# All 32 later output blocks in pairs of seven half products, and early units placed anew, in a fused attention and bilinear FFN kernel

## The chip, the cores and the metric

One core of one Trainium2 chip. The metric is device time in microseconds (us) of one execution of the whole kernel; the median of several runs is quoted. The profile is one execution, whose span (first to last instruction) is 1.7 to 1.8 us shorter than the time. All verdicts use runs of state fast.

## The reference, cut to what matters

```python
# q, k, v: (8 batches, 8 heads, 576, 64); phi: (8, 8, 576, 32); all f32
a = softmax(phi, axis=seq)                       # 32 memory slots per head
k_m, v_m = a^T k, a^T v                          # (32, 64) per head
attn = softmax(q k_m^T / 8) v_m
x = attn rearranged to (4608 tokens, 512)
out = ((x @ w_a) * (x @ w_b)) @ w_out            # d_ff = 1536; out: (4608, 512) f32
```

## The kernel before

Attention is never formed: v_m is folded into w_a and w_b for each batch (`fold`, tiles `pva` to `vab`), so that the two up projections (`pa`, `pb`) take the normalised scores `A` directly. ScalarE copies `pa` out, DVE multiplies it by `pb` into `ht` (f16). The down product takes `ht` in 36 blocks of 128 tokens. Four early ones are plain (12 products of 512 columns each, `po`). Later ones go in pairs: a pair of blocks, with d_ff and d_model halved, is a 2x2 times 2x2 block product that needs seven half products in place of eight, on sums of `ht` (`h_sums`, GpSimd or DVE) and of w_out (`w_sums`):

```python
def two_downs(self, cidx):                       # (cut to its order)
    y: a11*B11 -> u1      v: S1*T1 -> u5
    y += S2*T2 -> u2      v += S4*B22;  o1[:, NH:] = v + u2     (DVE)
    y += S3*T3;           o2[:, NH:] = y + u5                   (DVE)
    x: a12*B21;           o1[:, :NH] = x + u1                   (DVE), store o1
    y += a22*T4;          o2[:, :NH] = y                        (ACT), store o2
# each of the seven: 6 matmuls of 256 columns (KH = 6)
```

The last two blocks were left out of the pairs: block 34 is plain, block 35 is `last_down`, in two halves of 12 products of 256 columns, each stored as soon as it is ready, through SyncE and ScalarE:

```python
PAIRED = range(EARLY + PLAIN, BLOCKS - 2, 2)     # 15 pairs: blocks 4 to 33
def products(self):                              # (cut)
    for cidx in PAIRED[:-1]: yield from two_downs(self, cidx)
    yield from down(BLOCKS - 2)
    yield from two_downs(self, PAIRED[-1])
...
work.pull(work.ready - work.done)
last_down(B // 2 * NI - 1)
```

The chain of the next batch (`exp`, sums over k and v `ks vs` or `kv`, transposes `kt vt` or `kvt`, scores `sc`, `den`, `nr`, folds `v0 v1 v2` and their copies `x0 x1 x2`) is cut into units, and strings say in which slot (between two up products) each unit is issued; `a` and `b` are the folds of w_a and w_b, `hv` are half folds, `y3` is three early down products:

```python
ups(steps(0, 0, 4), slots(0, "- hv1a+hx1a - hv1b+hx1b - v1a+x1a - v1b+x1b"))
load(2)
ups(steps(0, 4, 12), slots(0, "- - - - v2a+x2a - v2b+x2b"))
chain(1, "exp0 exp1 y9 ks0 y3 kt0 qt0 qt1 y1 ks1 y3 kt1 s0 e0 ... y1 hv0a hx0a y2 hv0b hx0b y2")
```

Folds, sums, scores and the transposes of k and v run in tiled form (64 x 32, 32 x 32 or 128 x 32 of the array), ups and downs on the full array. Tiled work between full-array products is called an island below.

The softmax here doesn't subtract the row's maximum and nothing guards it: scores larger than these inputs give would overflow.

Of the kernel before, what the change touches and what calls it, by code (L numbers as in the profile page):

```python
# [8 lines left out]
F32 = mybir.dt.float32  # L9
F16 = mybir.dt.float16  # L10
AF = mybir.ActivationFunctionType
ALU = mybir.AluOpType

P = 128
# [4 lines left out]
def kernel(  # L19
# [381 lines left out]
    def down(cidx):  # L401

        po, bank = banks.take([P, d_model], F32, "po", hold=True)
        yield from down_part(po, bank, cidx, 0, NFF)

    def last_down(cidx):

        pair, c = divmod(cidx, NI)
        w = d_model // 2
        for x in range(2):  # L410
            cs = slice(w * x, w * (x + 1))
            po = banks.tile([P, w], F32, name="pl")
            o_sb = opool.tile([P, w], F32, name="o_sb")
            for i in range(NFF):
                nc.tensor.matmul(po, ht[:, i, P * c:P * (c + 1)], wo_sb[:, i, cs],
                                 start=(i == 0), stop=(i == NFF - 1))
            nc.scalar.mul(out=o_sb[:, :w // 2], in_=po[:, :w // 2], mul=1.0 / (CS * CS))
            nc.vector.tensor_scalar(out=o_sb[:, w // 2:], in0=po[:, w // 2:], scalar1=1.0 / (CS * CS), scalar2=None,
                                    op0=ALU.mult)
            for z, engine in enumerate((nc.sync, nc.scalar)):  # L420
                slot = 2 * c + z
                engine.dma_start(out=out_rows[2 * pair + slot // NI, slot % NI, :, cs],
                                 in_=o_sb[64 * z:64 * z + 64, :])

    EARLY = 4

    def early_downs():
# [28 lines left out]
    def sum_tokens(cidx, engine):  # L456

        h_sums[cidx] = spool.tile([P, 4, KH, P], F16, name="h_sums")
        t = [h_sums[cidx][:, x] for x in range(4)]
        (a11, a12), (a21, a22) = ([tokens_of(cidx + y, x) for x in range(2)] for y in range(2))  # L460
        for out, in0, in1, op in ((t[0], a21, a22, ALU.add), (t[1], t[0], a11, ALU.subtract),
                                  (t[2], a12, t[1], ALU.subtract), (t[3], a11, a21, ALU.subtract)):
            engine.tensor_tensor(out=out, in0=in0, in1=in1, op=op)  # L463
            yield

    def store(o_sb, cidx):
        pair, c = divmod(cidx, NI)
        for z in range(2):
            slot = 2 * c + z
            nc.sync.dma_start(out=out_rows[2 * pair + slot // NI, slot % NI], in_=o_sb[64 * z:64 * z + 64, :])  # L470

    def two_downs(self, cidx):
        S1, S2, S4, S3 = (h_sums[cidx][:, x] for x in range(4))
        T1, T2, T3, T4 = (w_sums[:, x] for x in range(4))
        (a11, a12), (a21, a22) = ([tokens_of(cidx + y, x) for x in range(2)] for y in range(2))
        scale = 1.0 / (CS * CS)

        def products(po, lhs, rhs, first=False):
            for i in range(KH):
                nc.tensor.matmul(po, lhs[:, i], rhs[:, i], start=first and i == 0,  # L480
                                 stop=i == KH - 1, skip_group_check=not first)
                if i < KH - 1:
                    yield

        def part(po, name):
            x = ppool.tile([P, NH], F32, name=name)
            nc.scalar.mul(out=x, in_=po, mul=scale)
            return x

        def plus(o, po, x):  # L490
            nc.vector.scalar_tensor_tensor(out=o, in0=po, scalar=scale, in1=x, op0=ALU.mult, op1=ALU.add)

        o1, o2 = (opool.tile([P, d_model], F32, name="o_sb") for _ in range(2))
        y, ybank = banks.take([P, NH], F32, "py", hold=True)
        yield from products(y, a11, quarter(0, 0), True)
        u1 = part(y, "u1")
        yield
        v, vbank = banks.take([P, NH], F32, "pv", hold=True)
        self.brim = True
        yield from products(v, S1, T1, True)  # L500
        u5 = part(v, "u5")
        yield
        yield from products(y, S2, T2)
        u2 = part(y, "u2")
        yield
        yield from products(v, S4, quarter(1, 1))
        banks.free(vbank)
        plus(o1[:, NH:], v, u2)
        self.brim = False
        yield  # L510
        yield from products(y, S3, T3)
        plus(o2[:, NH:], y, u5)
        yield
        x, xbank = banks.take([P, NH], F32, "px", hold=True)
        self.brim = True
        yield from products(x, a12, quarter(1, 0), True)
        banks.free(xbank)
        plus(o1[:, :NH], x, u1)
        store(o1, cidx)
        self.brim = False  # L520
        yield
        yield from products(y, a22, T4)
        banks.free(ybank)
        nc.scalar.mul(out=o2[:, :NH], in_=y, mul=scale)
        store(o2, cidx + 1)
        yield

    BLOCKS = B // 2 * NI
    LEAD = 24
    PLAIN = 0  # L530
    PAIRED = range(EARLY + PLAIN, BLOCKS - 2, 2)

    class Work:

# [7 lines left out]
            self.next_sum = next(self.sums)  # L542

        def products(self):
            for cidx in range(EARLY, EARLY + PLAIN):
                yield from down(cidx)
            for cidx in PAIRED[:-1]:
                yield from two_downs(self, cidx)
            yield from down(BLOCKS - 2)
            yield from two_downs(self, PAIRED[-1])  # L550

        def add_up(self):
            for n, cidx in enumerate(PAIRED):
                for x in range(4):
                    yield n, NFF * PLAIN + 7 * KH * n + KH * (x + 1)
                    if x == 0:
                        sums = sum_tokens(cidx, nc.gpsimd if n < len(PAIRED) - 1 else nc.vector)
                    next(sums)
            while True:
                yield len(PAIRED), 0  # L560

# [21 lines left out]
        def plan(self, tokens, slots, keep=24):  # L583

            n = min(max(0, tokens // P - PAIRED[0]) // 2, len(PAIRED))
            self.summed = n
            self.ready = NFF * min(PLAIN, tokens // P - EARLY) + 7 * KH * n + NFF * (tokens // P >= BLOCKS - 1)
            self.rate = max(0, self.ready - self.done - keep) / slots
            self.owed = 0.0
            self.sum_ahead()  # L590
# [27 lines left out]
    def ups(steps, side=()):  # L618

        side = iter(side)  # L620
        for step in steps:
            for _ in up(*step):
                work.advance()
                next(side, us[step[0]]["-"])()
        for f in side:
            work.advance()
            f()

    def steps(b, lo, hi):

        return [(b, i, (0, 1)) for i in range(lo, hi)]
# [37 lines left out]
    def chain(b, plan):  # L669


        for x in plan.split():
            if x[0] == "f":
                fill(int(x[1:]), 256)
            elif x[0] == "y":
                some(int(x[1:]))
            else:
                us[b][x]()
# [1 line left out]
    fill(16)  # L680
    chain(0, "exp0 exp1 ks0 f3 kt0 qt0 qt1 f14 s0 e0 ks1 f3 kt1 qt2 qt3 f6 den0 f4 s1 nr0 e1 f6 vs0 vs1 vt0 vt1 den1 f3 "
             "hv0a hx0a nr10 nr11 hv0b hx0b f4")
    ups(steps(0, 0, 4), slots(0, "- hv1a+hx1a - hv1b+hx1b - v1a+x1a - v1b+x1b"))
    load(2)
    ups(steps(0, 4, 12), slots(0, "- - - - v2a+x2a - v2b+x2b"))
    chain(1, "exp0 exp1 y9 ks0 y3 kt0 qt0 qt1 y1 ks1 y3 kt1 s0 e0 qt2 qt3 y6 den0 y2 s1 e1 nr0 y4 den1 y2 vs0 vs1 y1 vt0 vt1 nr1 y1 hv0a hx0a y2 hv0b hx0b y2")
    load(3)
    sum_weights()
    ups(steps(1, 0, 4), slots(1, "y1 hv1a+hx1a hv1b+hx1b y1 v1a+x1a v1b+x1b y3 y3"))
    ups(half_steps(1, 0, 4), slots(1, "- v2a+x2a+v2b+x2b+qt0' - exp0' - exp1'+qt1' - qt2'+kv'+km'+y9"))  # L690
    work.plan(S + HALF, 10)
    ups(half_steps(1, 1, 4), slots(2, "qt3 kvt - sc+e0+e1+den0 - nr0+den1+v0+x0a - - x0b+nr1 - v1+x1b+x1a -"))
    second = "v2_+x2a_+exp0 x2b_ - exp1 qt0+kv+km - qt1+kvt+qt2 qt3 sc+e0 - e1+v0+x0a x0b den0+v1+x1a nr0+L x1b+exp0' den1 - nr1+v2+x2a - x2b+exp1' qt0' kv'+qt1' km' - qt2'+kvt'+qt3'"
    every = "- sc+e0 e1 den0 v0+x0a+x0b - - nr0 exp0' - v1+x1a x1b+qt0' den1 - exp1' v2+x2a+x2b nr1+qt1' - kv'+km' qt2' kvt'+qt3' L - -"
    last = "sc+e0 - e1 - v0 x0b den1+x0a - den0 - nr0+v1+x1a nr1 x1b - - - - - - v2+x2a - - - x2b"
    for b in range(2, B):
        if b == 2:
            load(4)
# [4 lines left out]
            ups(half_steps(b, hf), side[NFF * hf:NFF * (hf + 1)] if hf == 0 else side[NFF:])  # L703
    work.plan(S * B, 1, 0)
    work.pull(work.ready - work.done)
    last_down(B // 2 * NI - 1)
# [1 line left out]
_INS = ['q', 'k', 'v', 'phi', 'moe_w_a', 'moe_w_b', 'moe_w_out']  # L708
_OUTS = [((4608, 512), 'float32')]
# [25 lines left out]
```

## Time and profile before

| | before |
|---|---|
| time, median of 3 | 247.81 us (247.73 to 247.85) |
| span of the profile | 246.4 us |
| first up product of batch 0 | 20.45 us |
| first up product of batch 1 | 49.63 us |
| last up product starts | 228.70 us |
| last down product ends | 242.14 us |
| last store lands | 245.28 us |

The positions are read from the timeline: the first `pa` row of a batch, the last `pb` row, and for the end the `pl` row (239.36 + 2.78) and the last store's issue with its time to landing.

### The profile page before, as it was taken

To read this page: it belongs to the slowest core of one execution; us is meant where nothing else is said; L and a number is where in the kernel's file an instruction comes from. 1 tells how busy PE (TensorE), PEld (TensorE's weight loads), DVE (VectorE), ACT (ScalarE), POOL (GpSimd) and SP (SyncE) were. 2 spreads that over 40 slices of the span, in tenths; PEclk is the share of its full clock that TensorE was granted. 3 is DMA by queue.
4 is the path that set the end of the run, shared out by engine and by line. 5 is a ranking of instruction groups with operands and counts; after the bars stand their busy time and mean duration, and the time that the engine had idled before them with its cause. 6 is when DMAs were issued, how large, how long until landed. Compare 5 with 4: busy or idle time off the path is not lost.

```text
span 246.4 us, 7681 instructions
## 1 busy us (share of the span) xinstructions
PE 234.4 (95%) x3049; PEld 167.1 (68%) x3049; DVE 166.5 (68%) x401; ACT 157.9 (64%) x409; POOL 151.1 (61%) x123
## 2 busy tenths in 40 slices
PE   7589999999998999999999999999999999999993
PEld 3354574456655857777787777877787787888782
DVE  3636794477959967876994649865995686756620
ACT  2247772578697489578856768588855877565330
POOL 8724233499799029892899759892849186936000
PEclk9999999999999999999999999999999999999999
DMA  6999999999979804973159732695120303033145
GB/s 198 210 198 206 211 252 207 255 220 271 233 183 207 160 4 108 238 127 85 33 149 208 174 85 45 167 207 145 32 56 3 88 7 82 10 78 71 43 104 128
DMA packets 26036, 33.82 MB, mean 137 GB/s; under 512 B 1936, under 2 KB 20368, under 8 KB 26000
## 3 DMA queue, kind: packets, MB, share of 16 engines
q0 software_dynamic: 19280, 22.71, 50.3%
q1 hardware_dynamic: 6288, 9.90, 16.3%
q10 hardware_dynamic: 432, 0.72, 0.8%
q8 instruction: 24, 0.39, 0.6%
q14 instruction: 12, 0.10, 0.1%
HBM read 42.47 MB, written 9.44 MB: 211 GB/s over the span
## 4 chain that ended last, share of the span: by engine, by line
PE 74%; DMA 17%; DVE 3%; POOL 2%; ACT 1%; issue 1%; ACTq 0%; DVEq 0%; POOLq 0%
PE pa L602 18%; PE pb L612 16%; PE py L480 15%; PE pv L480 8%; DMA phi_sb<-in_phi_dram 6%; DMA wo_sb<-in_moe_w_out_dram 6%; DMA wb_sb<-in_moe_w_b_dram 5%; PE pva L337 5%; PE px L480 4%; PE po L389 3%; PE pkv L213 2%; PE pD L314 1%; PE pscore L292 1%; PE pT L242 1%; POOL q_sb L90 1%
## 5 line engine op out<-in xcount | busy, mean ns | idle before, releaser
L615 DVE TENSOR_TENSOR ht<-a_sb,pb 128x288 f16<-128x288 f16 x192 | 82.9, 448 | 40.2 <-ACT a_sb L605 29.3
L605 ACT CAST a_sb<-pa 128x288 f16<-128x288 f32 x192 | 74.7, 405 | 31.6 <-PE pa L602 31.0
L602 PE MATMUL pa<-A,vab 128*128 128x288 f16 x384 | 76.5, 287 | 1.4 <-DVE A L325 1.4
L612 PE MATMUL pb<-A,vab 128*128 128x288 f16 x384 | 76.5, 286 | 0.2
L463 POOL TENSOR_TENSOR h_sums<-ht 128x768 f16<-128x768 f16 x28 | 45.9, 1640 | 34.0 <-DVE ht L615 34.0
L612 PEld LDWEIGHTS <-vab 128*128 128x128 f16 x384 | 37.0, 98 | 13.2 <-issue 1.9
L602 PEld LDWEIGHTS <-vab 128*128 128x128 f16 x384 | 34.5, 98 | 15.9 <-issue 9.1
L480 PEld LDWEIGHTS <-h_sums 128*128 128x128 f16 x360 | 35.1, 98 | 6.5 <-issue 0.4
L349 ACT CAST vab<-pva 128x512 f16<-128x512 f32 (+1 forms) x52 | 28.1, 558 | 10.0 <-PE pva L337 10.0
L349 DVE CAST vab<-pva 128x512 f16<-128x512 f32 (+1 forms) x52 | 32.8, 643 | 2.4 <-PE pva L337 2.0
L480 PEld LDWEIGHTS <-ht 128*128 128x128 f16 x270 | 26.4, 98 | 5.4 <-issue 0.2
L480 PE MATMUL py<-w_sums,h_sums 128*128 128x256 f16 x180 | 28.5, 272 | 0.0
L463 POOL TENSOR_TENSOR h_sums<-h_sums,ht 128x768 f16<-128x768 f16 x14 | 23.1, 1650 | 1.0
L463 POOL TENSOR_TENSOR h_sums<-ht,h_sums 128x768 f16<-128x768 f16 x14 | 23.0, 1642 | 1.0
L305 ACT ACTIVATE E<-pscore 128x288 f16<-128x288 f32 x32 | 11.4, 416 | 13.6 <-PE pscore L292 13.5
L325 POOL TENSOR_TENSOR A<-E,R 128x576 f16<-128x576 f16 x10 | 12.8, 1278 | 11.9 <-ACT R L323 11.6
L389 PE MATMUL po<-wo_sb,ht 128*128 128x512 f16 x60 | 16.0, 381 | 0.1
L480 PE MATMUL py<-wo_sb,ht 128*128 128x256 f16 x90 | 15.2, 273 | 0.0
L480 PE MATMUL pv<-w_sums,h_sums 128*128 128x256 f16 x90 | 15.2, 273 | 0.0
L204 DVE STREAM_TRANSPOSE qT<-q_sb 128x288 f32<-128x288 f32 x32 | 14.5, 463 | 0.6 <-DMA q_sb<-in_q_dram 0.6
L480 PE MATMUL py<-w_sums,ht 128*128 128x256 f16 x90 | 14.7, 272 | 0.1
L315 ACT ACTIVATE L<-pD 128x288 f32<-128x288 f32 x32 | 11.4, 413 | 5.0 <-PE pD L314 4.8
(66 smaller groups left out, 273.1 us busy)
## 6 DMA issues: line engine op xcount, KB each, us to landing
out_dram<-o_sb SPq DMA_DIRECT2D x70, 128.0 KB, 2.4
kv_sb<-in_v_dram POOLq DMA_DIRECT2D x7, 576.0 KB, 10.5
phi_sb<-in_phi_dram POOLq DMA_DIRECT2D x7, 576.0 KB, 4.6
kv_sb<-in_k_dram POOLq DMA_DIRECT2D x7, 576.0 KB, 8.2
q_sb<-in_q_dram POOLq DMA_DIRECT2D x6, 576.0 KB, 12.8
wo_sb<-in_moe_w_out_dram POOLq DMA_DIRECT2D x3, 512.0 KB, 17.4
q_sb<-in_q_dram POOLq DMA_DIRECT2D x4, 288.0 KB, 12.7
wa_sb<-in_moe_w_a_dram POOLq DMA_DIRECT2D x2, 512.0 KB, 14.8
```

What stands on the lines that cost most here:

```text
L204: nc.vector.transpose(out=t["qT"][:, hp, :].bitcast(F32), in_=qs[b][:, hp, :].bitcast(F32))
L305: nc.scalar.activation(out=Ev[:, g, :, z, :], in_=pss, func=AF.Exp, scale=1.0 / (8.0 * CS))
L325: engine.tensor_tensor(out=attn[b][:, g, sl], in0=t["E"][:, g, sl], in1=t["R", g][:, sl], op=ALU.mult)
L337: nc.tensor.matmul(t["pva", lo, z][g][0][32 * j:32 * j + 32, 0:hi - lo], t["kvT"][64 * r:64 * r + 64, 4 + g, M * j:M * j + M], w_sbs[z][64 ...
L349: engine_copy(out=vabs[b][z][:, g, lo:hi], in_=pva[:, 0:hi - lo])
L389: nc.tensor.matmul(po, ht[:, i, P * c:P * (c + 1)], wo_sb[:, i, :], start=(i == 0), stop=(i == NFF - 1))
L463: engine.tensor_tensor(out=out, in0=in0, in1=in1, op=op)
L480: nc.tensor.matmul(po, lhs[:, i], rhs[:, i], start=first and i == 0, stop=i == KH - 1, skip_group_check=not first)
L602: nc.tensor.matmul(pa, vab[0][:, g, fs], A[:, g, HALF * hf:HALF * (hf + 1)], start=(g == 0), stop=(g == 1))
L605: nc.scalar.copy(out=a_sb, in_=pa)
L612: nc.tensor.matmul(pb, vab[1][:, g, fs], A[:, g, HALF * hf:HALF * (hf + 1)], start=(g == 0), stop=(g == 1))
L615: nc.vector.tensor_tensor(out=ht[:, i, t0:t0 + HALF], in0=a_sbs[hf - hfs[0]], in1=pb, op=ALU.mult)
```

## The change

The intent: put the last two blocks into a sixteenth pair (48 products' worth becomes 42); let DVE sum the last two pairs; store the last pair in pieces; and place the early units anew, so that fewer tiled islands stand between full-array products and TensorE has work while inputs arrive. The diff, cut to its core:

```diff
-    def last_down(cidx):
-        ... (24 half-width products, four small stores)
-    def store(o_sb, cidx):
+    def store(o_sb, cidx, cs=slice(0, d_model), engines=(nc.sync, nc.sync)):
...
         plus(o2[:, NH:], y, u5)
+        if ends:                                   # ends: the last pair
+            store(o2, cidx + 1, slice(NH, d_model))
...
         nc.scalar.mul(out=o2[:, :NH], in_=y, mul=scale)
+        if ends:
+            store(o2, cidx + 1, slice(0, NH), (nc.sync, nc.scalar))
...
-    PAIRED = range(EARLY + PLAIN, BLOCKS - 2, 2)
+    PAIRED = range(EARLY, BLOCKS, 2)
-                        sums = sum_tokens(cidx, nc.gpsimd if n < len(PAIRED) - 1 else nc.vector)
+                        sums = sum_tokens(cidx, nc.gpsimd if n < len(PAIRED) - 2 else nc.vector)
...
-    ups(steps(0, 0, 4), slots(0, "- hv1a+hx1a - hv1b+hx1b - v1a+x1a - v1b+x1b"))
+    ups(steps(0, 0, 4), slots(0, "hv1a+hv1b hx1b+hx1a - - - v1a+x1a v1b x1b"))
-    ups(steps(0, 4, 12), slots(0, "- - - - v2a+x2a - v2b+x2b"))
+    ups(steps(0, 4, 12), slots(0, "- - - - v2a+x2a+v2b+x2b - -"))
-    chain(1, "... y1 ks1 y3 kt1 s0 e0 qt2 qt3 y6 den0 y2 s1 e1 nr0 y4 den1 y2 vs0 vs1 y1 vt0 vt1 nr1 y1 hv0a hx0a y2 hv0b hx0b y2")
+    chain(1, "... y1 y3 ks1 qt2 s0 e0 y6 kt1 qt3 den0 y3 s1 nr0 e1 y4 y2 den1 vs0 vs1 vt0 y1 vt1 nr1 hv0a hx0a hv0b y3 hx0b y2")
...  (slots of batches 2 to 7: units moved by one or two slots)
```

More of the change, by code (lines that the diff above doesn't have):

```diff
@@ L404, in down @@
         yield from down_part(po, bank, cidx, 0, NFF)
-    def last_down(cidx):
-        pair, c = divmod(cidx, NI)
-        w = d_model // 2
-        for x in range(2):
-            cs = slice(w * x, w * (x + 1))
-            po = banks.tile([P, w], F32, name="pl")
-            o_sb = opool.tile([P, w], F32, name="o_sb")
-            for i in range(NFF):
-                nc.tensor.matmul(po, ht[:, i, P * c:P * (c + 1)], wo_sb[:, i, cs],
-                                 start=(i == 0), stop=(i == NFF - 1))
-            nc.scalar.mul(out=o_sb[:, :w // 2], in_=po[:, :w // 2], mul=1.0 / (CS * CS))
-            nc.vector.tensor_scalar(out=o_sb[:, w // 2:], in0=po[:, w // 2:], scalar1=1.0 / (CS * CS), scalar2=None,
-                                    op0=ALU.mult)
-            for z, engine in enumerate((nc.sync, nc.scalar)):
-                slot = 2 * c + z
-                engine.dma_start(out=out_rows[2 * pair + slot // NI, slot % NI, :, cs],
-                                 in_=o_sb[64 * z:64 * z + 64, :])
     EARLY = 4
@@ L469, in store @@
             slot = 2 * c + z
-            nc.sync.dma_start(out=out_rows[2 * pair + slot // NI, slot % NI], in_=o_sb[64 * z:64 * z + 64, :])
+            engines[z].dma_start(out=out_rows[2 * pair + slot // NI, slot % NI, :, cs], in_=o_sb[64 * z:64 * z + 64, cs])
     def two_downs(self, cidx):
@@ L476, in two_downs @@
         scale = 1.0 / (CS * CS)
+        ends = cidx == PAIRED[-1]
         def products(po, lhs, rhs, first=False):
@@ L524, in two_downs @@
         nc.scalar.mul(out=o2[:, :NH], in_=y, mul=scale)
-        store(o2, cidx + 1)
+        if ends:
+            store(o2, cidx + 1, slice(0, NH), (nc.sync, nc.scalar))
+        else:
+            store(o2, cidx + 1)
         yield
@@ L529 @@
     LEAD = 24
-    PLAIN = 0
-    PAIRED = range(EARLY + PLAIN, BLOCKS - 2, 2)
+    PAIRED = range(EARLY, BLOCKS, 2)
     class Work:
@@ L544, in products @@
         def products(self):
-            for cidx in range(EARLY, EARLY + PLAIN):
-                yield from down(cidx)
-            for cidx in PAIRED[:-1]:
+            for cidx in PAIRED:
                 yield from two_downs(self, cidx)
-            yield from down(BLOCKS - 2)
-            yield from two_downs(self, PAIRED[-1])
         def add_up(self):
@@ L554, in add_up @@
                 for x in range(4):
-                    yield n, NFF * PLAIN + 7 * KH * n + KH * (x + 1)
+                    yield n, 7 * KH * n + KH * (x + 1)
                     if x == 0:
-                        sums = sum_tokens(cidx, nc.gpsimd if n < len(PAIRED) - 1 else nc.vector)
+                        sums = sum_tokens(cidx, nc.gpsimd if n < len(PAIRED) - 2 else nc.vector)
                     next(sums)
@@ L586, in plan @@
             self.summed = n
-            self.ready = NFF * min(PLAIN, tokens // P - EARLY) + 7 * KH * n + NFF * (tokens // P >= BLOCKS - 1)
+            self.ready = 7 * KH * n
             self.rate = max(0, self.ready - self.done - keep) / slots
@@ L682 @@
              "hv0a hx0a nr10 nr11 hv0b hx0b f4")
-    ups(steps(0, 0, 4), slots(0, "- hv1a+hx1a - hv1b+hx1b - v1a+x1a - v1b+x1b"))
+    ups(steps(0, 0, 4), slots(0, "hv1a+hv1b hx1b+hx1a - - - v1a+x1a v1b x1b"))
     load(2)
-    ups(steps(0, 4, 12), slots(0, "- - - - v2a+x2a - v2b+x2b"))
-    chain(1, "exp0 exp1 y9 ks0 y3 kt0 qt0 qt1 y1 ks1 y3 kt1 s0 e0 qt2 qt3 y6 den0 y2 s1 e1 nr0 y4 den1 y2 vs0 vs1 y1 vt0 vt1 nr1 y1 hv0a hx0a y2 hv0b hx0b y2")
+    ups(steps(0, 4, 12), slots(0, "- - - - v2a+x2a+v2b+x2b - -"))
+    chain(1, "exp0 exp1 y9 ks0 y3 kt0 qt0 qt1 y1 y3 ks1 qt2 s0 e0 y6 kt1 qt3 den0 y3 s1 nr0 e1 y4 y2 den1 vs0 vs1 vt0 y1 vt1 nr1 hv0a hx0a hv0b y3 hx0b y2")
     load(3)
     sum_weights()
-    ups(steps(1, 0, 4), slots(1, "y1 hv1a+hx1a hv1b+hx1b y1 v1a+x1a v1b+x1b y3 y3"))
-    ups(half_steps(1, 0, 4), slots(1, "- v2a+x2a+v2b+x2b+qt0' - exp0' - exp1'+qt1' - qt2'+kv'+km'+y9"))
+    ups(steps(1, 0, 4), slots(1, "- hv1a+hx1a hv1b+hx1b+y1 - v1a+x1a y3+v1b x1b y3"))
+    ups(half_steps(1, 0, 4), slots(1, "- v2a+x2a+v2b+x2b+qt0' - - qt1'+exp0'+qt2' exp1' - kv'+km'+y9"))
     work.plan(S + HALF, 10)
-    ups(half_steps(1, 1, 4), slots(2, "qt3 kvt - sc+e0+e1+den0 - nr0+den1+v0+x0a - - x0b+nr1 - v1+x1b+x1a -"))
-    second = "v2_+x2a_+exp0 x2b_ - exp1 qt0+kv+km - qt1+kvt+qt2 qt3 sc+e0 - e1+v0+x0a x0b den0+v1+x1a nr0+L x1b+exp0' den1 - nr1+v2+x2a - x2b+exp1' qt0' kv'+qt1' km' - qt2'+kvt'+qt3'"
-    every = "- sc+e0 e1 den0 v0+x0a+x0b - - nr0 exp0' - v1+x1a x1b+qt0' den1 - exp1' v2+x2a+x2b nr1+qt1' - kv'+km' qt2' kvt'+qt3' L - -"
-    last = "sc+e0 - e1 - v0 x0b den1+x0a - den0 - nr0+v1+x1a nr1 x1b - - - - - - v2+x2a - - - x2b"
+    ups(half_steps(1, 1, 4), slots(2, "- kvt qt3 sc+e0+e1+den0 - nr0+den1+v0+x0a - - x0b+nr1 - v1+x1b x1a"))
+    second = "v2_+x2a_+exp0 x2b_ exp1 - qt0+kv+km - qt1+qt2 kvt+qt3 sc+e0 - e1+v0+x0a den0+x0b v1+x1a nr0+L x1b+exp0' den1 - nr1+v2+x2a - x2b+exp1' - qt0'+kv'+qt1' km' - qt2'+kvt'+qt3'"
+    every = "- sc+e0 e1 den0 v0+x0a+x0b - - nr0+exp0' - - v1+x1a qt0' x1b+den1 exp1' - v2+x2a+x2b nr1+qt1' kv'+km' qt2' - qt3' - kvt'+L -"
+    last = "sc+e0 - e1 - v0+x0b - x0a den1 - - den0 v1+x1b x1a+nr0 - - - - nr1+v2+x2a - - - - - x2b"
     for b in range(2, B):
@@ L705 @@
     work.pull(work.ready - work.done)
-    last_down(B // 2 * NI - 1)
 _INS = ['q', 'k', 'v', 'phi', 'moe_w_a', 'moe_w_b', 'moe_w_out']
```

## The prediction

> **What bounds the kernel now.** I read the page first, then the busy time by stretches, the waits of TensorE, the chain of waits in order of time, and last the timeline around each place that the change touches. The page, parts 1 and 2:
>
> ```profile
> PE 234.4 (95%) x3049; PEld 167.1 (68%) x3049; DVE 166.5 (68%) x401; ACT 157.9 (64%) x409; POOL 151.1 (61%) x123
> ...
> PE   7589999999998999999999999999999999999993
> ...
> PEclk9999999999999999999999999999999999999999
> ```
>
> TensorE is busy 95% of the span; only the first three slices, the thirteenth and the last are thin. "Busy" is not "at its peak", so the stretches come next (columns: busy us of PE, PEld, DVE, ACT, POOL with counts, clock, DMA share, GB/s):
>
> ```profile
> 30.00:40.00 10.00, 10.00 (x118) 6.18 (x117) 6.84 (x18) 6.23 (x16) 3.67 (x5) 1.00 1.19 236
> ...
> 70.00:80.00 10.00, 8.99 (x105) 5.83 (x103) 9.10 (x18) 8.75 (x22) 9.51 (x8) 1.00 1.01 195
> ...
> 120.00:140.00 20.00, 20.00 (x289) 15.39 (x287) 14.16 (x36) 13.07 (x38) 18.35 (x14) 1.00 0.83 173
> ```
>
> Up to about 70 us the DMA engines are full (share above 1); from 80 us on TensorE alone is full and DVE and ACT have a third free. Its waits are few (engine, line, waited for: total us, times, longest):
>
> ```profile
> PE pT L274 <- DVE kvm L266: 1.9, 3, 1.5
> PE pa L602 <- DVE A L325: 1.4, 2, 1.0
> ...
> PE pD L314 <- ACT E L305: 0.6, 1, 0.6
> PE pT L242 <- DVE rep L233: 0.4, 1, 0.4
> ```
>
> The first is in the start-up chain, which the diff leaves alone. The chain of waits (start us, us) shows what paces the first 48 us: arriving inputs.
>
> ```profile
> 18.19 15.25 DMA phi_sb<-in_phi_dram
> 33.44 14.95 DMA wo_sb<-in_moe_w_out_dram
> 48.43 0.59 PE po L389 x2
> ```
>
> So the third part of wo lands at 33.44 + 14.95 = 48.39 and an early down product (po) starts on it at 48.43: time won by TensorE before that point is worth only what the arrivals allow.
>
> **What the Trainium skill says.** (1) "TensorE: Matmul & The Clock Gate", section "Back-to-back issue gap": a warm matmul of N columns takes N/2.4 + 2.5 ns of the stream, which is 109 ns for 256 columns, 122 for 288, 216 for 512. The trace agrees: six py products take 0.66 us in the chain of waits (110 ns each), four pa of 288 take 0.49 us (33.76 to 34.25 below). (2) "TensorEngine Tiling (Array Packing)", section "Key Properties": "Changing tiling mode (not just tile) drains the TensorE". The trace gives the size:
>
> ```profile
> 23.01 0.65 PE L612 MATMUL pb<-A,vab 128*128 128x288 f16 x4
> 23.60 0.30 PE L337 MATMUL pva<-wb_sb,kvT 64*32 64x256 f16 x8
> ...
> 24.39 0.89 PE L612 MATMUL pb<-A,vab 128*128 128x288 f16 x4
> ...
> 26.98 0.66 PE L602 MATMUL pa<-A,vab 128*128 128x288 f16 x4
> 27.75 0.87 PE L612 MATMUL pb<-A,vab 128*128 128x288 f16 x4
> ...
> 33.76 0.65 PE L612 MATMUL pb<-A,vab 128*128 128x288 f16 x4
> 34.25 0.65 PE L602 MATMUL pa<-A,vab 128*128 128x288 f16 x4
> ```
>
> Four pb followed by a full-array pa take 0.49 us; four pb followed by a tiled pva take 0.59. So each switch costs 0.10 us, an island of tiled work two of them. (3) "SBUF — State Buffer", section "Who interferes with whom": a DVE instruction with two SBUF inputs contends with a GpSimd instruction that reads SBUF, and the later one blocks. The one long wait in the middle agrees: DVE's A = E*R takes 1.42 us at 73.70 while a GpSimd h_sums runs (73.17 to 74.81), against 0.46 us at 70.65 with none running. (4) "DMA: Bandwidth & Descriptors", section "Anatomy of one DMA": about 2.0 us of each DMA is fixed; the last 64 KB stores land 2.0 us after issue here.
>
> **The change, part by part.**
>
> *A. Folds of batch 0 (20 to 36 us).* hv1a and hv1b become one island (two switches fewer, 0.2 us), and come earlier, as does v1b. That takes away the pauses where pb waits for its copied weights: the pb row at 24.39 lasts 0.89 instead of 0.65, the pa row at 26.98 takes 0.77 to the next instead of 0.49, the pb row at 27.75 lasts 0.87: 0.24 + 0.28 + 0.22 = 0.74. So TensorE reaches v2a at 30.02 - 0.94 = 29.1. But v2b now follows v2a at once, and it reads the last third of wb, issued at 14.38; the longest landing of a wb piece is 16.2 us, so it is there at 30.55 (GpSimd, waiting for the same landing to issue its next load, goes on at 30.84). TensorE then waits some 1.2 us for it. From the pb row at 30.36 to the end of batch 0 at 36.21 there are 5.85 us, of which the old v2b island was 0.44; now 30.6 + 0.32 + 5.41 = 36.33: **+0.1**, the whole gain of A lost at the arrival.
>
> *B. Chain of batch 1 (36.2 to 49.6).* ks1 and s0 touch, vs1 and vt0 touch, vt1, hv0a and hv0b touch, kt1 stands alone: 19 switches become 17 (-0.19). The wait for wo's third part (pva at 47.91 to po at 48.43, 0.52 against the 0.24 of the next such pair, 0.28) goes, as 32 products instead of 32 plus the fold stand ahead and hv0b now comes in front of it. Against it vt1 is followed by hv0a with no product between; PE transposes, DVE copies (0.2), PE folds: before, 0.48 us from vt1 to hv0a with a product inside, so some +0.25 idle. One product more moves into the chain and out of the next stage (nothing net). **-0.2.**
>
> *C. Batch 1's ups and batch 2's chain (49.6 to 76).* The islands stay four, one and two. exp and q transposes come in other slots. ACT runs without a pause from 58.6 to 62.6, so moving an exp inside that does nothing much. qt3 now follows the kvT copy on DVE; before, scores started (66.98) just as that copy ended (66.27 + 0.54), so now they wait for about a transpose, 0.47, less what DVE gets ahead by the earlier qt2: +0.1 to +0.3. The two waits of 0.6 (sc, e0, e1, den0 still in one slot) and 1.0 us (nr1 still right after the last ht, which also starts the GpSimd sum) stay. Call it **+0.1**.
>
> *D. Batches 3 to 7.* As many islands, as many instructions; TensorE has nothing to gain from other slots except the 0.4 us wait for rep near 103, whose kv', km', kvt' keep their distance. **0.**
>
> *E. The end.* Two plain blocks (12 products of 512 and 24 of 256, worth 48 of 256) become a pair of 42: six fewer, 6 x 109 = -0.65 us. The lines here (timeline of the end):
>
> ```profile
> 230.51 0.55 DVE L463 TENSOR_TENSOR h_sums<-ht 128x768 f16<-128x768 f16 x1
> ...
> 230.57 0.82 PE L480 MATMUL px<-wo_sb,ht 128*128 128x256 f16 x6
> ...
> 231.45 0.81 PE L480 MATMUL py<-w_sums,ht 128*128 128x256 f16 x6
> ...
> 242.23 0.28 ACT L417 ACTIVATE o_sb<-pl 128x128 f32<-128x128 f32 x1 [1.03 <-PE pl L415]
> ...
> 242.64 1.19 SPq L422 DMA_DIRECT2D out_dram<-o_sb  x2
> ```
>
> px to py takes 0.88 instead of 0.66: DVE's sums sit in front of the read that frees py. A second pair now has its sums on DVE there: +0.2. And SyncE needs about 0.6 us to issue one store. Before, it is already behind (the next-to-last small store waits for it until 242.64). After, five stores (half of o2, all of o1, a quarter of o2) come within the last 1.3 us of products: the last one would be issued about 1.5 us after the last product instead of 1.1 us (242.14 to 243.28): +0.2 to +0.4. Together **-0.2**.
>
> Sum: 0.1 - 0.2 + 0.1 + 0 - 0.2 = -0.2; with a little credit for the smaller stalls I cannot place, I predict 247.5 us.
>
> **Rivals.** (1) Arrivals do not bind, because the loads land earlier than I think or the merged folds avoid them: then A is worth -0.9 and a further -0.2 for the v2 island, B and E as above: about 246.2. For it: the DMA queue is steady and only one fold stands on the gate; against: the 30.55 landing is DMA-paced, and the wo landing caps it again. (2) DVE's order bites: scores of batch 2 and of batch 3 (kvt now a slot nearer to its scores, qt3 behind it) wait for transposes, rep near 103 waits longer: up to 248.4. Against: ahead of batch 3's scores the work list is run down (18 products from 84.67), 2 us of cover. (3) The 1.0 us wait for A at 74 goes because A no longer meets the GpSimd sum: 246.5. Against: both hang on the same last ht. (4) At the end SyncE is quicker than 0.6 us a store: 247.1.
>
> **Range and chances.** The terms are each some 0.3 us uncertain and the gate at 30.55 counts 1 us, so eight times in ten 246.4 to 248.3. A 2% change is 5 us, more than all waits after 20 us together: faster 0.02, same 0.97, slower 0.01.
>
> **What would show it.** A: a hole in PE just before the fold that reads wb, near 29.3 to 30.6, and batch 0's ups ending at 36.2 to 36.4; if they end near 35.3, A's gate is wrong. B: no PE wait for wo at 48.4, a hole of 0.2 to 0.3 before hv0a, first pa of batch 1 near 49.6. C: pD and A waits still 0.6 and 1.0. D: equal busy time and equal count of instructions from 110 to 220. E: PE's last product 0.4 to 0.5 earlier relative to the last up; five SP stores in a row behind it. If the whole is under 246 the arrivals were no gate; if over 248.3 DVE's order was the bound.

## The result, and the profile after

The changed kernel took 247.8 us (median of 4, 247.72 to 248.0), against 247.77 for before in the same comparison. The ratio is 1.0005, 95% interval 0.9987 to 1.0022: no difference. Ratios here are the mean time of one kernel's fast runs over that of the other's of the same rounds, so they are not quite the ratio of the medians. Executions over 1.5% slower than the fastest of the same kernel are left out of the means. A later repeat on another occasion gave 0.9992 (0.9979 to 1.0005).

The page after, parts 1 and 2, and TensorE's waits:

```profile
PE 233.6 (95%) x3055; PEld 167.6 (68%) x3055; DVE 169.9 (69%) x406; ACT 158.2 (64%) x410; POOL 150.9 (61%) x123
...
PE   7788899999998999999999999999999999999992
```

```profile
PE pa L584 <- DVE A L325: 1.5, 2, 1.1
PE pw L151 <- DVE warm L120: 1.3, 1, 1.3
PE pb L594 <- DVE vab L349: 0.7, 1, 0.7
...
PE pD L314 <- ACT E L305: 0.5, 1, 0.5
PE pT L242 <- DVE rep L233: 0.4, 1, 0.4
```

TensorE is busy 0.8 us less, the thin thirteenth slice is as thin as before, and the waits for A, E and rep stand as they stood. One is new: `pb` waits 0.7 us for `vab`. Where it is, in the timeline of TensorE around 30 us:

```profile
26.58 0.65 PE L584 MATMUL pa<-A,vab 128*128 128x288 f16 x4
27.07 0.28 PE L594 MATMUL pb<-A,vab 128*128 128x288 f16 x1
28.09 0.54 PE L594 MATMUL pb<-A,vab 128*128 128x288 f16 x3 [0.73 <-DVE vab L349]
...
30.03 0.41 PE L337 MATMUL pva<-wa_sb,kvT 64*32 64x512 f16 x8
30.61 0.41 PE L337 MATMUL pva<-wb_sb,kvT 64*32 64x512 f16 x8 [0.18 <-ACT a_sb L587]
...
36.36 2.10 PE L389 MATMUL po<-wo_sb,ht 128*128 128x512 f16 x9
```

x1b was left a slot behind v1b, so its DVE half stands behind two `ht` products (26.61 to 27.43 on DVE) and the second matmul of `pb` waits 0.9 us beyond its turn. Then the wb fold starts at 30.61, 0.58 us after the wa fold instead of 0.22: the last part of wb landed at 30.57. The line names ACT, whose `a_sb` was done at 30.59, just as late; but in folds_early below, ACT was done at 29.42, wb landed at 30.41 and the same fold started at 30.45, so the landing is the gate. It is not always there: over the fourteen profiles this landing came between 29.64 and 30.58, and with the same slots in slots_only (29.64) the fold started at 30.25, straight behind the wa fold. Batch 0's ups end at 36.36, against 36.21 before. The chain of batch 1 ends like this:

```profile
47.95 0.24 PE L274 MATMUL pT<-ident,kvm 128*32 128x128 f16 x4
48.12 0.70 PE L337 MATMUL pva<-wa_sb,kvT 64*32 64x256 f16 x8
48.55 0.39 PE L337 MATMUL pva<-wb_sb,kvT 64*32 64x256 f16 x8
48.87 1.25 PE L389 MATMUL po<-wo_sb,ht 128*128 128x512 f16 x5
49.95 0.65 PE L584 MATMUL pa<-A,vab 128*128 128x288 f16 x4
```

The fold hv0a takes 0.43 us to the next fold instead of 0.12: it waits for DVE's copy of vt1, with no product in between. `po` no longer waits for wo. The first up of batch 1 comes at 49.95 with one `po` (0.22 us) more behind it, so level with before within 0.1 us.

The end, first the products and DVE's sums, then SyncE's stores:

```profile
230.11 0.55 DVE L444 TENSOR_TENSOR h_sums<-ht 128x768 f16<-128x768 f16 x1
230.17 0.82 PE L462 MATMUL px<-wo_sb,ht 128*128 128x256 f16 x6
...
231.05 0.81 PE L462 MATMUL py<-w_sums,ht 128*128 128x256 f16 x6
...
235.04 0.82 PE L462 MATMUL px<-wo_sb,ht 128*128 128x256 f16 x6
...
235.89 0.81 PE L462 MATMUL py<-w_sums,ht 128*128 128x256 f16 x6
...
240.56 0.81 PE L462 MATMUL py<-w_sums,ht 128*128 128x256 f16 x6
241.41 0.38 ACT L508 ACTIVATE o_sb<-py 128x256 f32<-128x256 f32 x1 [2.23 <-PE py L462]
```

```profile
240.53 3.03 SPq L451 DMA_DIRECT2D out_dram<-o_sb  x5
```

px to py takes 0.88 and 0.85 us where DVE sums stand in the way (twice now), 0.68 in the last pair where none do. SyncE issues five stores without a gap of note, 3.03 us for five; the last quarter of the output was ready at 241.80, but its SyncE half was issued only at 243.02.

The sum over the span, from positions of the same up product in both traces:

| | before | after | after minus before, growing |
|---|---|---|---|
| first up of batch 0 | 20.45 | 20.20 | -0.25 (start-up, same instructions) |
| batch 0's ups end | 36.21 | 36.36 | +0.15 |
| first up of batch 2 | 73.88 | 73.75 | -0.13 |
| half way through batch 3 (up product 336 of 768) | 116.81 | 116.83 | +0.02 |
| end of batch 6 (672) | 208.33 | 207.93 | -0.40 |
| last up | 228.70 | 228.30 | -0.40 |
| last product ends | 242.14 | 241.38 | -0.76 |
| last store lands | 245.28 | 245.01 | -0.27 |

So 0.76 us are won at the last product, and half a microsecond is given back between it and the landing. The 0.25 us of start-up are no gain of the change: over the fourteen profiles the first up product came between 19.93 and 20.94 us, with the same instructions in front of it. Where TensorE is full, profiles repeat far better: from up product 336 to 672 it is 91.52 and 91.54 us in the two profiles with the old slots, and 91.10 or 91.11 in all twelve with the new ones.

### The profile page after: what moved, and what is told of

It is laid out like the page before. It is cut to its first block, busy times and chain, and to the rows that moved or that the text cites. A ratio compares the mean times of both kernels' runs of the same rounds, so it can differ in the third digit from the quotient of the medians.

```text
span 246.2 us, 7701 instructions
## 1 busy us (share of the span) xinstructions
PE 233.6 (95%) x3055; PEld 167.6 (68%) x3055; DVE 169.9 (69%) x406; ACT 158.2 (64%) x410; POOL 150.9 (61%) x123
## 4 chain that ended last, share of the span: by engine, by line
PE 87%; DVE 5%; DMA 2%; ACT 2%; issue 2%; DVEq 0%; ACTq 0%
PE pa L584 20%; PE pb L594 18%; PE py L462 16%; PE pv L462 8%; PE pva L337 5%; PE po L389 5%; PE px L462 4%; DMA ht<-in_k_dram 2%; PE pkv L213 2%; PE pD L314 2%; PE pscore L292 2%; PE pw L151 2%; PE pk L256 1%; DVE ht L597 1%; PE pT L242 1%
## 5 line engine op out<-in xcount | busy, mean ns | idle before, releaser
L462 PEld LDWEIGHTS <-h_sums 128*128 128x128 f16 x384 | 37.4, 98 | 6.9 <-issue 0.4
L462 PEld LDWEIGHTS <-ht 128*128 128x128 f16 x288 | 28.1, 98 | 5.6 <-issue 0.4
L462 PE MATMUL py<-w_sums,h_sums 128*128 128x256 f16 x192 | 30.3, 272 | 0.0
L462 PE MATMUL py<-wo_sb,ht 128*128 128x256 f16 x96 | 16.0, 273 | 0.0
L462 PE MATMUL pv<-w_sums,h_sums 128*128 128x256 f16 x96 | 16.0, 273 | 0.0
L469 ACT ACTIVATE u<-py 128x256 f32<-128x256 f32 x32 | 12.4, 387 | 5.2 <-PE py L462 5.0
L462 PE MATMUL py<-w_sums,ht 128*128 128x256 f16 x96 | 15.5, 272 | 0.1
L462 PE MATMUL px<-wo_sb,ht 128*128 128x256 f16 x96 | 15.4, 273 | 0.0
```

Source lines behind the costliest of these rows:

```text
L462: nc.tensor.matmul(po, lhs[:, i], rhs[:, i], start=first and i == 0, stop=i == KH - 1, skip_group_check=not first)
L469: nc.scalar.mul(out=x, in_=po, mul=scale)
```

## The experiments

All ran correctly; each is timed against the kernel before on the same chip, in five rounds. Theory: the new slots meet arriving inputs and win next to nothing early; the six products fewer are won, and the pile of stores at the end gives them back. Rivals: the slots cost what the end gained; or DVE's sums alone ate it.

**1. The end alone, and the slots alone.** `end_only` is the changed kernel with every slot string of before; `slots_only` is the kernel before with every slot string of the change.

```diff
 # end_only
-    ups(steps(0, 0, 4), slots(0, "hv1a+hv1b hx1b+hx1a - - - v1a+x1a v1b x1b"))
+    ups(steps(0, 0, 4), slots(0, "- hv1a+hx1a - hv1b+hx1b - v1a+x1a - v1b+x1b"))
     ... (and the eight other strings; slots_only is the reverse)
```

> The changed kernel's end (sixteen pairs, no plain blocks, its own last stores) with all slots as before the change. Theory (six products fewer are real, but SyncE's queue of stores gives them back): TensorE's last product ends 0.4 to 0.5 us earlier than before (near 241.7), the last store is issued some 1.6 us after that product instead of 1.1, and the time is 247.6 to 247.8. Rival 1 (the new slots had cost what the end gained): 247.1 to 247.3.

> The new slots with the end as before. Theory: batch 0's ups end near 36.3 and the first pa of batch 1 is near 49.9 (with one po more in front of it), so nothing is won there; a gain of about 0.3 us grows between 120 and 220 us; at the end it is kept because the stores there are as before: 247.4 to 247.6. Rival 1 (the new slots cost time): 248.1 or more.

| | time, us | ratio to before (95%) | last up to last product's end | last product's end to landing |
|---|---|---|---|---|
| before | 248.0 (11 runs) | | 13.44 | 3.14 |
| end_only | 248.2 | 1.0009 (0.9997 to 1.0021) | 13.07 | 3.64 |
| slots_only | 247.45 | 0.9986 (0.9973 to 0.9998) | 13.44 | 3.11 |

The end alone wins 0.37 us of products and loses 0.50 us behind them: nothing is left, as the theory had it (the 248.2 us is outside the 247.6 to 247.8 named, but the kernel before ran at 248.0 in this call). Rival 1 falls: the slots alone are not slower but 0.14% faster, some 0.35 us. The profile of slots_only places most of it between 116 and 208 us (its lead grows from 0.35 to 0.77), while end_only keeps a constant 0.17 to 0.19 over all that stretch. The prediction had not foreseen that gain; some two thirds of it stand in the kv sums of batches 5 to 7, here those near 153 us, before and then after:

```profile
153.52 1.03 PE L213 MATMUL pkv<-kv_sb,exp_sb 64*32 64x192 f16 x72
```

```profile
152.62 0.94 PE L213 MATMUL pkv<-kv_sb,exp_sb 64*32 64x192 f16 x72
```

The 72 matmuls take 0.09 us less in each of three batches, because one gap of 80 ns near their end is gone. What made that gap the profile does not say. Most of the rest stands between up products 592 and 608 (0.12 us), where two `pD` products, of the denominators, take 0.35 us to the next `pa` before and 0.25 after:

```profile
191.52 0.41 PE L314 MATMUL pD<-E,ones 128*128 128x288 f16 x2
191.87 0.42 PE L602 MATMUL pa<-A,vab 128*128 128x288 f16 x2
```

```profile
192.16 0.41 PE L314 MATMUL pD<-E,ones 128*128 128x288 f16 x2
192.41 0.41 PE L584 MATMUL pa<-A,vab 128*128 128x288 f16 x2
```

Why that one waits is open too.

**2. The last stores over three queues.**

```diff
-            store(o2, cidx + 1, slice(NH, d_model))
+            store(o2, cidx + 1, slice(NH, d_model), (nc.sync, nc.scalar))
-        store(o1, cidx)
+        store(o1, cidx, engines=(nc.sync, nc.gpsimd) if ends else (nc.sync, nc.sync))
```

> The changed kernel, the last pair's six stores over three queues (SyncE, ScalarE, GpSimd) in place of five on SyncE. Theory (SyncE's queue is the bound after the last product): the product stream is unchanged, the last landing comes 0.5 to 0.8 us sooner, time 247.0 to 247.3. Rival 2 (the sums on DVE ate the gain, or the landing itself takes this long): no change, 247.7 to 247.9.

247.43 us, ratio to before 0.998 (0.9968 to 0.9993); the repeat of the changed kernel had 0.9992, so some 0.3 us are won, not 0.6 (the two intervals overlap; the positions below are the better evidence). SyncE's row in the new trace, and the last stores' time to landing (columns: KB, us from issue to landing), in the changed kernel and here:

```profile
240.40 1.76 SPq L451 DMA_DIRECT2D out_dram<-o_sb  x3
```

```profile
out_dram<-o_sb SPq DMA_DIRECT2D x1, 64.0 KB, 2.0
```

```profile
out_dram<-o_sb SPq DMA_DIRECT2D x1, 64.0 KB, 2.8
out_dram<-o_sb ACTq DMA_DIRECT2D x1, 64.0 KB, 2.9
```

The last store is issued at 241.69 instead of 243.02, 0.45 us behind the last product instead of 1.64. But it then takes 2.9 us to land instead of 2.0. Its twin on SyncE's own queue takes 2.8, so ScalarE's queue is not the reason; the stores overlap more, and the 16 DMA engines are 0.89 busy from 242 to 243 us, against 0.38 in the changed kernel, whose full stretch comes later (1.00 from 243 to 244). Product to landing falls from 3.63 only to 3.37 us. So the queue of SyncE was the first thing that the stores waited for, and behind it stands the transfer itself. The theory was half right: of the 0.5 us given back, this takes 0.26 us away again.

**3. The last sums later.**

```diff
-                    yield n, 7 * KH * n + KH * (x + 1)
+                    yield n, 7 * KH * n + KH * (x + 1) + (12 if n > 13 else 0)
```

> The changed kernel; the four DVE sums of each of the last two pairs are issued 12 products later, so that none stands in front of DVE's read of the py bank. Theory: the two pauses of 0.2 us between px and py (230.7 and 235.6) go, the last product ends 0.4 us earlier behind the last up (12.7 us instead of 13.1), and since SyncE's stores move with it the time is about 0.4 us less than the changed kernel: 247.4. Rival (the pauses come from the reads themselves, not from the sums): pauses and time unchanged, 247.8.

247.41 us, ratio to before 0.9977 (0.9964 to 0.999). The pauses are gone (230.12 to 230.79 and 234.78 to 235.46 are 0.67 and 0.68):

```profile
230.12 0.82 PE L462 MATMUL px<-wo_sb,ht 128*128 128x256 f16 x6
230.79 0.81 PE L462 MATMUL py<-w_sums,ht 128*128 128x256 f16 x6
...
234.78 0.82 PE L462 MATMUL px<-wo_sb,ht 128*128 128x256 f16 x6
235.46 0.82 PE L462 MATMUL py<-w_sums,ht 128*128 128x256 f16 x6
```

From the last up to the last product's end it is 12.69 us instead of 13.08, 0.39 as expected. In the changed kernel DVE ran a sum from 230.11 to 230.66 and only behind it, to 231.00, the read that TensorE was waiting for; that sum could as well be issued 12 products later.

**4. Batch 0's folds without the two pauses.**

```diff
-    ... "hv1a+hv1b hx1b+hx1a - - - v1a+x1a v1b x1b"
+    ... "hv1a+hv1b hx1b+hx1a - - - v1a+x1a v1b+x1b -"
-    ... "- - - - v2a+x2a+v2b+x2b - -"
+    ... "- - - - v2a+x2a - v2b+x2b"
```

> The changed kernel with x1b in v1b's slot and v2a, v2b in two slots again, so that neither the wait for x1b's copy (0.9 us at 27 us) nor the wait for the last part of wb (0.35 us at 30.6) is there. Theory (arrivals pace the first 48 us): batch 0's ups end about 0.9 us earlier (near 35.4), but TensorE then waits for k (37.4) and for the second and third parts of wo (41.3 and 48.3), and the first pa of batch 1 is at most 0.5 us earlier (49.5); time 247.4 to 247.7. Rival (no gate): first pa near 49.0, time 246.9.

247.2 us, ratio 0.997 (0.9958 to 0.9982). Batch 0's ups end at 35.21, 1.15 us earlier than in the changed kernel (0.27 of it start-up), and then TensorE waits for the second part of wo:

```profile
40.42 0.45 PE L292 MATMUL pscore<-qT,kvT 32*32 32x288 f16 x16
41.21 1.02 PE L389 MATMUL po<-wo_sb,ht 128*128 128x512 f16 x4 [0.34 <-DMA wo_sb<-in_moe_w_out_dram]
```

In this profile the first up of batch 1 came at 49.20, which looks like 0.75 us won. One profile would mislead: the same folds in three later kernels gave 49.37, 49.65 and 49.88 (mean of four 49.53), and the changed kernel's folds in eight profiles 49.58 to 49.95 (mean 49.76). So of the 0.60 us won at the end of batch 0's ups (means of the same profiles, 36.17 and 35.56) about 0.24 are left at the first up of batch 1. The times allow more: 0.997 against 0.9992 would be 0.5 us, and 247.2 us lies between the 247.4 to 247.7 of the theory and the rival's 246.9. That arrivals take part of the gain is shown by the wait; how much of it, these runs do not settle, as the spread from run to run is as large as the effect.

**5. The waits in the middle: first tries.** `one_sum_later` is the edit of 3 with `n == 1`, meant to move the GpSimd sums of the second pair out of the way of DVE's A. `den_kvt_later` moves den0 of batch 2 and kvt of batch 4 one slot on, to put work into the waits for E and rep.

```diff
-    ups(half_steps(1, 1, 4), slots(2, "- kvt qt3 sc+e0+e1+den0 - nr0+den1+v0+x0a ..."))
+    ups(half_steps(1, 1, 4), slots(2, "- kvt qt3 sc+e0+e1 den0 nr0+den1+v0+x0a ..."))
-    second = "... qt2'+kvt'+qt3'"
+    second = "... qt2'+qt3'"          # and kvt in the first slot of the next batch
```

> The changed kernel; the GpSimd sums of the second pair alone are issued 12 products later, past DVE's A = E*R of batch 2. Theory (the 1.07 us that TensorE waits for A near 74 us is a collision of a two-input DVE instruction with a GpSimd instruction that reads SBUF): that A takes 0.5 us instead of 1.4, the wait falls to 0.2 us or less, time about 0.9 us less, 246.9. Rival (A is late because ScalarE is): wait and time unchanged.

> The changed kernel; den0 of batch 2 one slot after its scores, kvt of batch 4 one slot later. Theory (both pauses, 0.55 us for E near 68 and 0.4 to 0.8 us for rep near 103, are only a matter of too little work in between): both go, time 1.0 to 1.3 us less, 246.5 to 246.8. Rival (ScalarE and DVE are the bound there, so the wait comes back at the next consumer): less than 0.4 us.

one_sum_later: 247.76 us, ratio 0.9988 (0.9974 to 1.0002), and a failed experiment: GpSimd began that sum at 72.68, at once behind the last `ht` as in the changed kernel, and A took 1.47 us. The later place in the program delayed nothing, since the engine had nothing else in its queue. It told nothing of the collision.

den_kvt_later: 248.19 us, ratio 1.0009 (0.9995 to 1.0022): the rival was right. At 68 us the wait for E went, and 0.31 us at the next pD and some 0.25 in the fold came instead; from the first up of batch 1 to that of batch 2 it took 23.76 us instead of 23.79. At 103 the wait for rep went and a longer one came:

```profile
103.26 0.55 PE L242 MATMUL pT<-ident,rep 128*128 128x128 f16 x6
...
105.82 0.45 PE L292 MATMUL pscore<-qT,kvT 32*32 32x288 f16 x24 [1.20 <-DVE kvT L243]
```

With kvt moved, the scores follow it too closely and wait 1.20 us for DVE's copy; from there to half way through batch 3 it takes 43.53 us instead of 43.08. DVE has no pause between 103.2 and 105.8 in this run, so it is the bound in those slots, and not TensorE's order.

**6. A without the collision.** One GpSimd copy of a column of A, behind the loads and in front of the sums in GpSimd's order, so that the sums cannot begin before A is made:

```diff
         if b == 2:
             load(4)
+            nc.gpsimd.tensor_copy(out=after_A, in_=attn[2][:, 1, 0:1])
```

> The changed kernel; one GpSimd copy of a single column of A (batch 2) in front of the second pair's sums, so that GpSimd cannot start them before DVE has made A. (The run one_sum_later moved only the place in the program; GpSimd started the sums at the same moment, as their data was there, and so told nothing.) Theory (collision of DVE's two-input A with the GpSimd sum): A takes 0.5 us instead of 1.48, TensorE's wait near 74 us falls from 1.07 to 0.2 or less, first pa of batch 3's side of that wait 0.9 us earlier, time 0.9 us less than the changed kernel (246.9). Rival (A is slow or late by itself): wait and time unchanged.

246.75 us, ratio to before 0.9955 (0.9943 to 0.9967), against 0.9992 for the changed kernel: 0.9 us, as expected. The changed kernel, and then this one:

```profile
73.05 1.67 POOL L444 TENSOR_TENSOR h_sums<-ht 128x768 f16<-128x768 f16 x1
...
73.57 1.48 DVE L325 TENSOR_TENSOR A<-E,R 128x576 f16<-128x576 f16 x1
...
75.10 0.28 PE L584 MATMUL pa<-A,vab 128*128 128x288 f16 x1 [1.07 <-DVE A L325]
```

```profile
73.47 0.46 DVE L326 TENSOR_TENSOR A<-E,R 128x576 f16<-128x576 f16 x1
73.63 0.62 PE L585 MATMUL pa<-A,vab 128*128 128x288 f16 x2
...
73.99 0.19 POOL L682 COPY after_A<-A 128x1 f16<-128x1 f16 x1 [1.04 <-DVE A L326]
...
74.13 1.64 POOL L445 TENSOR_TENSOR h_sums<-ht 128x768 f16<-128x768 f16 x1
```

The same DVE instruction takes 0.46 us instead of 1.48, and TensorE no longer waits. The sums start 1.1 us later, and nobody waits for them: from the first up of batch 2 to half way through batch 3 it takes 42.06 us instead of 43.08. The rival (A late or slow by itself) falls.

**7. Together.** `best3` is 2, 3 and 4 on the changed kernel, `best4` adds 6; `all_five` was an earlier sum, with one_sum_later and den_kvt_later in it. `after_again` is the changed kernel once more.

> All of it on the changed kernel: folds as in folds_early, last stores over three queues, last sums later, second pair's sums later, den0 and kvt later. Theory (each is a pause of TensorE and from 49 us on TensorE is the bound, so they add): 0.6 + 0.6 + 0.4 + 0.9 + 1.1 = 3.6 us less, 244.2 (244 to 245). Rival (a pause that is closed in one place opens in the next): 246.0 or more.

> The changed kernel with the three edits that worked: folds of folds_early, last stores over three queues, sums of the last two pairs 12 products later. Theory (independent pauses): 0.6 + 0.4 + 0.4 = 1.4 us less than the changed kernel, 246.4, ratio to before 0.994 to 0.996. Rival (they overlap): 247.2.

> best3 with the edit of a_first. Theory: a further 0.9 us, 245.5, ratio to before 0.991. Rival: as best3.

> The changed kernel once more, on the same chip as the three others: as on record, 247.8, ratio to before 0.999 to 1.002.

| | time, us | ratio to before (95%) |
|---|---|---|
| after_again | 247.62 | 0.9992 (0.9979 to 1.0005) |
| all_five | 247.25 | 0.9973 (0.9959 to 0.9987) |
| best3 | 247.07 | 0.9959 (0.9947 to 0.9971) |
| best4 | 246.06 | 0.9926 (0.9914 to 0.9937) |

(One run of best3, 252.18, is not among the fast ones.) all_five missed its 244.2 by 3 us: two of its parts did nothing or harm, and the folds and stores were worth less than I had put down. best3 wins 0.33% on after_again, 0.8 us of the expected 1.4, since the folds give a quarter microsecond and the stores a quarter. best4 adds 0.8 us from A (245.5 was expected, so the sum falls short by the same half microsecond as best3) and beats both kernels: 1.9 us below the one before, 0.7%, clear of the noise though under the 2% that counts as faster. Its last product ends 12.70 us behind the last up, and the last landing is 3.38 us behind that.

## Why the prediction was right, by its own steps

The time was 247.8, inside 246.4 to 248.3 and 0.3 from the 247.5 named; no change was forecast and none came. The parts were of mixed quality. As measured in the pair of profiles they are +0.15, -0.05, -0.23, -0.27 and +0.13, together -0.27 (the last landing), against +0.1, -0.2, +0.1, 0 and -0.2: three are off by about 0.3 and their errors cancelled, so that the sum came so near is partly luck.

- **A (+0.1).** Measured +0.15, with v2b at 30.61 where 30.6 was named. But the step that got there was half wrong: I let the pauses for copied weights vanish and put the whole hole before v2b. They did not vanish; the one at 27 us grew to 0.9, as x1b was left in its own slot, and only 0.35 was spent before v2b. The gate on wb made both ways end at the same time. Rival 1 (no gate) was real in part: in slots_only wb was there in time, but then batch 0's ups ended at 35.98, only 0.23 earlier, as the pauses were still there. folds_early bears out the larger point, that little of A would pass the arrivals: about 0.25 us by the positions, 0.5 by the times.
- **B (-0.2).** From the end of batch 0 to the first up of batch 1 it is 13.59 less one `po`, 13.37, against 13.42: -0.05. The wait for wo went and the hole before hv0a is 0.29, both as said; unforeseen was a second hole of 0.17, where vt0 directly follows vs1 (0.29 from one to the other at 47.17, with a switch of 0.09 in it).
- **C (+0.1).** It was -0.2. No scores waited for qt3: the earlier qt2 probably gave DVE enough lead (not tested), and rival 2 fell with that. The gain is elsewhere, in two folds of wb in batch 1's first ups, which I had taken for unchanged: with hv1b it is 0.31 us to the next product before and 0.23 after, with v1b 0.52 (54.27 to 54.79) and 0.34 (54.98 to 55.32), now that a `po` product stands behind the one and three in front of the other (the cause of the pauses was not tested). The waits of 0.55 and 1.07 stayed, as said. Rival 3 named the second one's worth (246.5); a_first, which removed it, ran 246.75.
- **D (0).** It was -0.27: 0.15 lost up to half way through batch 3, which I cannot place, then 0.42 won. The instructions are the same, but slots differ: 0.27 of the gain is in the kv sums of three batches and 0.10 at one `pD`. The claim that other slots have nothing to give once TensorE is full was wrong.
- **E (-0.2).** The term with the clearest test. Products: -0.45 said, -0.36 measured, with the second pause of 0.2 where it was said; last_sums_later shows that the sums make it. Stores: +0.2 to +0.4 said, +0.49 measured. Together +0.13 instead of -0.2. The step said that the last store would be issued 1.5 us behind the last product; it was 1.64. That this is SyncE's issue time is only part of it, as stores_spread shows: with the queue gone, the landing takes 0.9 us longer. Rival 4 (SyncE quicker than 0.6 us a store) falls with the 3.03 us for five.

What became of the expected gain, then: the six products are won (0.65 us), 0.2 goes to a DVE read behind a sum, the rest to the last stores. The slots alone win about 0.35 us by time, at the edge of the noise; the 0.42 us between up products 336 and 672 recur in every profile with these slots.

## What to carry to other kernels

Work taken off the bounding engine just before the end is worth only what the tail lets through: count the stores that become ready in the last microsecond, and keep every other instruction out from in front of the reads that free a bank. A longer duration of one instruction of an always equal kind (1.48 us where its twin takes 0.46) is a collision to look for, and putting one engine's free work behind it by a data dependency was worth more here than the whole rearrangement. Before an early stage is packed tighter, find when its inputs land, and take more than one profile: here the start alone moved by up to 1 us, while a stretch in which TensorE was full repeated within 0.02 us. Small gains are best read from such a stretch.

## What the Trainium skill lacked or had wrong

- "TensorEngine Tiling (Array Packing)" says that a change of tiling mode drains TensorE but gives no size: here each switch costs about 0.10 us. From one tiled form to another it seems to cost the same: 36 `pk` products (64 x 32) take 0.62 us to the next product, whether that is a full-array `po` (38.39 to 39.01 after) or a 32 x 32 score (40.95 to 41.57).
- "TensorE: Matmul & The Clock Gate", section "Back-to-back issue gap", gives N/2.4 + 2.5 ns, the formula of the prediction, for a matmul on its own, and about 131 ns a matmul for a real stream of 512 columns. The prediction took the formula for the stream; the traces agree with it there, and not with the 131 ns: `po` products of 512 columns follow each other every 0.216 us, products of 256 every 0.110.
- "DMA: Bandwidth & Descriptors" gives about 2.0 us as the fixed part of a DMA that GpSimd issues (section "Anatomy of one DMA — SWDGE (gpsimd) path"); the stores here are issued by SyncE and ScalarE. The last 64 KB store took 2.0 us behind four others on one queue and 2.9 us when the six were spread over three queues. For the issue time of a store on SyncE I found no figure there: here it is 0.47 to 0.60 us each, 3.03 us for five.
- "SBUF — State Buffer" (section "Who interferes with whom") has the collision of DVE and GpSimd right: 1.48 against 0.46 us, ending 0.3 us behind the GpSimd sum.
- No page that I read says how much the start of a kernel varies: first up product between 19.93 and 20.94 us in fourteen profiles.
